# Attention backward for one query row: a broadcast moved into the score bank, the two sums given banks of their own, and the joins of their rows moved one slot later

## The chip, the cores and the metric

The kernel runs on one core of a Trainium2 chip. The metric is device time in microseconds (us), lower is better. Engines: PE (matrix multiply; PEld is its weight load, which overlaps it: in the kernel before 911 us of it beside 1146 us of multiplies, in a span of 1306 us), DVE (vector), ACT (scalar), POOL and SP (here they send the stores and the loads). A "head" is one of the 64 pairs of batch and head; a "slot" is one eighth of a head's work.

## The reference

For each of 64 heads: one query row, 8192 keys and values of length 128, all bf16. Wanted are the forward output and the gradients of q, k and v.

```python
B, H, Sq, Sk, D = 2, 32, 1, 8192, 128

def _fwd_reference(q, k, v):
    scale = q.shape[-1] ** -0.5
    scores = jnp.einsum("bhqd,bhkd->bhqk", q, k) * scale
    p = _softmax(scores, axis=-1)
    return jnp.einsum("bhqk,bhkd->bhqd", p, v)

def reference(q, k, v, grad_out):
    _out, _vjp = jax.vjp(lambda q, k, v: _fwd_reference(q, k, v), q, k, v)   # shortened
    return (_out, *_vjp(grad_out))
```

K and V are read once and their gradients written once: 64 x 2 x 2 MB = 268.5 MB each way. With one query row there is little arithmetic per byte.

## The kernel before

Each slot of head `i` transposes 16 tiles of keys (slots 0 to 3) or values (4 to 7) on PE, copies them out on ACT, and multiplies them with q or the output gradient. Beside it run the previous head's sums (`acc`, PE), the masks that pick the right rows (`pick`, DVE), the join of those rows (`join`, PE, then ACT), and the outer products that make the gradients of k and v (`outer`, DVE), which are then stored. Cuts are marked.

```python
    kvp = ctx.enter_context(tc.tile_pool(name="kv", bufs=6))
    outp = ctx.enter_context(tc.tile_pool(name="outp", bufs=4))
    ps_m = ctx.enter_context(tc.tile_pool(name="ps_m", bufs=2, space=bass.MemoryType.PSUM))
    # ...
    def broadcast(i):                       # q and grad_out of head i on all partitions
        qbp = ps_m.tile([P, 2, D], F32, tag="m", name="qbp")
        pin(nc.tensor.matmul(qbp[:], lhsT=ident_bf[:BH, i : i + 1].to_broadcast([BH, P]),
                             rhs=qd_nat[:], start=True, stop=True))
        h.qb = work.tile([P, 2, D], BF16, tag="qb", name="qb")
        pin(nc.vector.tensor_copy(out=h.qb[:], in_=qbp[:]))
    # ...
    def acc(i, w, c):                       # w=1: values, w=0: keys
        if c == 0:
            h.acc[w] = ps_m.tile([P, QT * D], F32, tag="m", name="acc")
        # ... 4 matmuls of 32 columns x 512
    def pick(i, w): ...                     # DVE: full = acc * diag (0.68 us), sel = reduce(full) (1.04 us)
    def join(i, w): ...                     # PE: acc[:, 0:1] = sel.T @ ones;  ACT: copy to oT / dqT
    # ...
    for g in range(SL * (BH + 2)):          # SL = 8 slots, NCH = 4
        i, s = divmod(g, SL)
        # ... loads
        if live:
            if s == 1: begin_s(i)
            if s == 2: broadcast(i)
            # ...
            ev = transpose_chunk(i, s)
        # ...
        if one: acc(i - 1, 1 if s < NCH else 0, s % NCH)
        if one and s == NCH + 1: join(i - 1, 1)
        if two and s == 1:       join(i - 2, 0)
        # ... scores
        if one and s == NCH: pick(i - 1, 1)
        if two and s == 0:   pick(i - 2, 0)
        # ... outer products: four for each of the two results, then a 2 MB store
```

The broadcast and the two sums share two PSUM banks through one tag. A join stands one slot after its `pick`.

## Time and profile before

| | before |
|---|---|
| time, median of 3 runs | 1306.98 us (1305.65 to 1308.0) |
| PE busy / DVE / ACT | 1146 / 952 / 975 us of a span of 1305.7 |
| bytes moved | 268.5 MB in, 268.5 MB out |
| mean granted PE clock | 0.837 |

From the page of the kernel before: the span in 40 slices (clock in tenths, share of busy DMA engines in tenths, rate), the queues with packets, MB and share of 16 engines, and the chain of work that ended last.

```profile
PEclk9999977788898878778888878689787977886896
DMA  9999999999999999999999999999999999999976
GB/s 375 398 427 428 426 428 427 428 429 425 428 429 427 421 424 424 421 417 422 427 425 422 423 421 406 417 415 427 425 418 425 402 413 411 417 395 423 419 330 266
...
q0 software_dynamic: 18432, 268.44, 49.3%
q1 hardware_dynamic: 19184, 268.51, 48.7%
q8 instruction: 149, 2.44, 0.7%
...
DMA 39%; issue 25%; PE 21%; ACT 10%; DVE 3%; POOL 1%; SPq 0%; POOLq 0%; ACTq 0%
```

The DMA engines are marked busy nearly everywhere; the rate is flat near 428 GB/s at first and ragged later.

Four lines of the list of waits of the kernel before (who waited for whom: total us, times, longest):

```profile
PE acc L337 <- DVE sel L327: 69.5, 109, 4.6
...
PE tp L167 <- DMA kt<-in_k_dram: 39.7, 33, 2.6
...
PE qbp L135 <- ACT dqT L342: 24.0, 62, 0.8
...
PE tp L167 <- DMA vt<-in_v_dram: 9.8, 11, 1.2
```

PE waits 69.5 us for the masks and 24.0 us for the bank in which it puts the broadcast, 93.5 us together, and 49.5 us for loads. The timeline of the kernel before shows both waits of one head (start, duration, instruction, in brackets PE's idle time before it):

```profile
653.22 0.69 DVE L319 TENSOR_TENSOR full<-acc,diag 128x512 f32<-128x512 f32 x1
...
653.95 1.04 DVE L327 TENSOR_REDUCE sel<-full 128x128 f32<-128x512 f32 x1
...
655.04 0.38 PE L337 MATMUL acc<-ones_f,sel 128*128 128x1 f32 x2 [0.59 <-DVE sel L327]
...
655.84 0.28 ACT L342 ACTIVATE dqT<-acc,rls 128x1 bf16<-128x1 f32 x1
...
656.17 0.27 PE L135 MATMUL qbp<-qd_nat,ident_bf 64*128 64x256 bf16 x1 [0.34 <-ACT dqT L342]
```

And longer stretches of it (us, busy time by engine, granted clock, DMA share, GB/s):

```profile
100.00:400.00 300.00, 266.36 (x4526) 212.39 (x4523) 225.32 (x394) 229.99 (x182) 16.52 (x31) 0.86 1.01 428
400.00:700.00 300.00, 270.32 (x4444) 215.01 (x4442) 220.81 (x389) 227.05 (x180) 15.99 (x30) 0.82 1.01 423
700.00:1000.00 300.00, 266.96 (x4422) 212.63 (x4420) 219.07 (x382) 226.73 (x179) 15.46 (x29) 0.84 1.00 419
1000.00:1200.00 200.00, 181.06 (x2918) 143.91 (x2915) 143.00 (x254) 148.05 (x119) 10.67 (x20) 0.80 1.00 411
```

The share stays at 1.0 while the rate sinks from 428 to 411 GB/s.

### The profile page before, as it was taken

To read this page: it belongs to the slowest core of one execution; us is meant where nothing else is said; L and a number is where in the kernel's file an instruction comes from. 1 tells how busy PE (TensorE), PEld (TensorE's weight loads), DVE (VectorE), ACT (ScalarE), POOL (GpSimd) and SP (SyncE) were. 2 spreads that over 40 slices of the span, in tenths; PEclk is the share of its full clock that TensorE was granted. 3 is DMA by queue.
4 is the path that set the end of the run, shared out by engine and by line. 5 is a ranking of instruction groups with operands and counts; after the bars stand their busy time and mean duration, and the time that the engine had idled before them with its cause. 6 is when DMAs were issued, how large, how long until landed. Compare 5 with 4: busy or idle time off the path is not lost.

```text
span 1305.7 us, 41737 instructions
## 1 busy us (share of the span) xinstructions
PE 1146.0 (88%) x19076; PEld 911.5 (70%) x19076; DVE 951.7 (73%) x1680; ACT 974.7 (75%) x769; POOL 69.5 (5%) x136
## 2 busy tenths in 40 slices
PE   7999889999889989999988989988988899999983
PEld 6777777777667777777767767776767677777762
DVE  2888876777777767678777776777676867776776
ACT  7888877787777777768777767778786777876871
POOL 0000000000000000000000000000000000000000
PEclk9999977788898878778888878689787977886896
DMA  9999999999999999999999999999999999999976
GB/s 375 398 427 428 426 428 427 428 429 425 428 429 427 421 424 424 421 417 422 427 425 422 423 421 406 417 415 427 425 418 425 402 413 411 417 395 423 419 330 266
DMA packets 37793, 539.62 MB, mean 413 GB/s; under 512 B 4464, under 2 KB 4464, under 8 KB 4976
## 3 DMA queue, kind: packets, MB, share of 16 engines
q0 software_dynamic: 18432, 268.44, 49.3%
q1 hardware_dynamic: 19184, 268.51, 48.7%
q8 instruction: 149, 2.44, 0.7%
q14 instruction: 28, 0.23, 0.0%
HBM read 268.47 MB, written 268.47 MB: 411 GB/s over the span
## 4 chain that ended last, share of the span: by engine, by line
DMA 39%; issue 25%; PE 21%; ACT 10%; DVE 3%; POOL 1%; SPq 0%; POOLq 0%; ACTq 0%
DMA kt<-in_k_dram 31%; PE tp L167 13%; ACT ev L169 9%; DMA vt<-in_v_dram 8%; PE acc L303 3%; PE sw L179 2%; POOL out_dram L369 1%; PE dpw L179 1%; DVE sel L327 1%; DVE full L319 1%; PE qbp L135 1%; PE acc L337 0%; ACT dqT L342 0%; DVE mp L191 0%; DVE ob L357 0%
## 5 line engine op out<-in xcount | busy, mean ns | idle before, releaser
L169 ACT COPY ev<-tp 128x2048 bf16<-128x2048 bf16 x512 | 939.0, 1871 | 303.9 <-PE tp L167 303.6
L357 DVE TENSOR_TENSOR ob<-qb,pair 128x2048 bf16<-128x2048 bf16 x512 | 611.3, 1216 | 0.0
L167 PE MATMUL tp<-ident_bf,kt 128*128 128x128 bf16 x4096 | 361.6, 259 | 39.7 <-DMA kt<-in_k_dram 39.7
L167 PEld LDWEIGHTS <-kt 128*128 128x128 bf16 x4096 | 311.5, 118 | 80.1 <-DMA kt<-in_k_dram 42.6
L179 PEld LDWEIGHTS <-ev 128*128 128x128 bf16 x8192 | 255.9, 99 | 100.0 <-issue 61.2
L167 PE MATMUL tp<-ident_bf,vt 128*128 128x128 bf16 x4096 | 291.8, 228 | 9.8 <-DMA vt<-in_v_dram 9.8
L167 PEld LDWEIGHTS <-vt 128*128 128x128 bf16 x4096 | 251.0, 103 | 10.8 <-DMA vt<-in_v_dram 10.8
L179 PE MATMUL sw<-qdT,ev 128*128 128x1 bf16 x4096 | 143.5, 165 | 1.0 <-ACT ev L169 1.0
L179 PE MATMUL dpw<-qdT,ev 128*128 128x1 bf16 x4096 | 141.2, 164 | 1.5 <-ACT ev L169 1.5
L191 DVE TENSOR_REDUCE mp<-sw 128x1 f32<-128x64 f32 x64 | 14.4, 225 | 169.9 <-PE sw L179 169.9
L327 DVE TENSOR_REDUCE sel<-full 128x128 f32<-128x512 f32 x128 | 133.1, 1040 | 4.4
L369 POOL DMA_DIRECT2D out_dram<-ob x128 | 68.4, 534 | 1227.8 <-DVE ob L357 637.4
L337 PEld LDWEIGHTS acc<-ones_f,sel 128*128 128x128 f32 x256 | 42.0, 206 | 111.6 <-DVE sel L327 105.5
L337 PE MATMUL acc<-ones_f,sel 128*128 128x1 f32 x256 | 52.8, 276 | 69.9 <-DVE sel L327 69.5
L319 DVE TENSOR_TENSOR full<-acc,diag 128x512 f32<-128x512 f32 x128 | 87.5, 684 | 0.0
L230 DVE CUSTOM_DVE_ANT_0 junk<-E_f,dpw 128x64 bf16<-128x64 f32 x64 | 14.0, 219 | 58.7 <-PE dpw L179 58.7
L303 PE MATMUL acc<-vt,E_pad_110 128*32 128x512 bf16 x336 | 42.7, 499 | 0.0
L303 PE MATMUL acc<-vt,E_pad_109 128*32 128x512 bf16 x352 | 42.3, 473 | 0.0
L135 PE MATMUL qbp<-qd_nat,ident_bf 64*128 64x256 bf16 x64 | 19.6, 307 | 24.0 <-ACT dqT L342 24.0
L303 PE MATMUL acc<-vt,E_pad_111 128*32 128x512 bf16 x336 | 39.7, 463 | 0.0
L303 PE MATMUL acc<-kt,dS_pad_112 128*32 128x512 bf16 x352 | 36.4, 408 | 0.5 <-DVE dS_pad_112 L276 0.5
L303 PE MATMUL acc<-kt,dS_pad_113 128*32 128x512 bf16 x336 | 35.1, 408 | 0.0
(61 smaller groups left out, 458.3 us busy)
## 6 DMA issues: line engine op xcount, KB each, us to landing
out_dram<-ob POOLq DMA_DIRECT2D x128, 2048.0 KB, 28.0
vt<-in_v_dram SPq DMA_DIRECT2D x64, 2048.0 KB, 30.6
kt<-in_k_dram SPq DMA_DIRECT2D x63, 2048.0 KB, 29.2
kt<-in_k_dram SPq DMA_DIRECT2D x4, 512.0 KB, 5.4
qd_nat<-in_q_dram SPq DMA_DIRECT2D x1, 16.0 KB, 1.9
qd_nat<-in_grad_out_dram SPq DMA_DIRECT2D x1, 16.0 KB, 2.0
out_dram<-dqn SPq DMA_DIRECT2D x1, 16.0 KB, 4.9
out_dram<-on SPq DMA_DIRECT2D x1, 16.0 KB, 6.4
```

Of the source, the lines that this page charges most:

```text
L135: nc.tensor.matmul(qbp[:], lhsT=ident_bf[:BH, i : i + 1].to_broadcast([BH, P]), rhs=qd_nat[:], start=True, stop=True,)
L167: pin(nc.tensor.transpose(tp[:, t, :], src[:, n0 + t, :], ident_bf[:]))
L169: pin(nc.scalar.copy(out=ev[:], in_=tp[:]))
L179: nc.tensor.matmul(dst[:, n0 + t : n0 + t + 1], lhsT=ev[:, t, :], rhs=qdT[:, w, i : i + 1], start=True, stop=True,)
L191: pin(nc.vector.reduce_max(out=h.mp[:], in_=h.s, axis=AX.X))
L230: nc.vector.tensor_tensor_reduce(out=junk[:], in0=h.E_f[:], in1=h.dp, scale=1.0, scalar=0.0, op0=ALU.mult, op1=ALU.add, accum_out=h.ld[:, ...
L303: nc.tensor.matmul(h.acc[w][g : g + CW, :], lhsT=wts[:, n0 : n0 + CW], rhs=rows[:, n0 : n0 + QT, :].rearrange("p n d -> p (n d)"), start=( ...
L319: nc.vector.tensor_tensor(out=full[0:NR], in0=h.acc[w][0:NR].rearrange("p (n d) -> p n d", n=QT), in1=diag[0:NR], op=ALU.mult,)
L327: nc.vector.reduce_sum(out=h.sel[0:NR], in_=full[0:NR].rearrange("p n d -> p d n"), axis=AX.X)
L337: nc.tensor.matmul(h.acc[w][:, 0:1], lhsT=h.sel[0:NR], rhs=ones_f[0:NR, 0:1], start=True, stop=True)
L357: nc.vector.tensor_tensor(out=h.ob[:, n0 : n0 + CH, :].rearrange("p n (e t) -> p n e t", t=2), in0=h.qb[:, w, :] .rearrange("p (e t) -> p ...
L369: store_eng.dma_start(out=dst[i], in_=h.ob[:])
```

## The change

Its intent is to take both waits from PE: the broadcast goes into spare columns of the score bank, at slot 0; each sum gets a bank of its own; the joins come two slots after the mask instead of one.

```diff
-    ps_m = ctx.enter_context(tc.tile_pool(name="ps_m", bufs=2, space=bass.MemoryType.PSUM))
+    ps_m = ctx.enter_context(tc.tile_pool(name="ps_m", bufs=1, space=bass.MemoryType.PSUM))
...
-        qbp = ps_m.tile([P, 2, D], F32, tag="m", name="qbp")
         pin(
             nc.tensor.matmul(
-                qbp[:],
+                h.qbp,
...
-        pin(nc.vector.tensor_copy(out=h.qb[:], in_=qbp[:]))
+        pin(nc.vector.tensor_copy(out=h.qb[:], in_=h.qbp))
...
-        sw = ps_sdp.tile([P, NT + P + 1], F32, tag="s", name="sw")
+        sw = ps_sdp.tile([P, NT + P + 1 + 2 * D], F32, tag="s", name="sw")
+        h.qbp = sw[:, NT + P + 1 :].rearrange("p (w d) -> p w d", w=2)
...
-            h.acc[w] = ps_m.tile([P, QT * D], F32, tag="m", name="acc")
+            h.acc[w] = ps_m.tile([P, QT * D], F32, tag=f"acc{w}", name="acc")
...
-            if s == 1:
+            if s == 0:
                 begin_s(i)
-            if s == 2:
                 broadcast(i)
...
-        if one and s == NCH + 1:
+        if one and s == NCH + 2:
             join(i - 1, 1)
-        if two and s == 1:
+        if two and s == 2:
             join(i - 2, 0)
```

(Cut: two helper tiles at the start and the end take the new tags.)

## The prediction

> **What bounds the kernel now.** It moves 268.5 MB in and 268.5 MB out. The page's slices show the DMA engines nine tenths busy or more in 38 of 40; in 50-us windows their share is 0.99 to 1.01 from 50 to 1250 us, at a flat 427 to 428 GB/s from 100 to 400 us. [...] no 50-us window passes 428. So transfers set the pace: at 428 GB/s 537 MB take 1255 us. The rest of the 1306 us is the first 10 us (252 GB/s), a tail of some 48 us after the last head's keys land (stores only, VectorE full, about 20 us of transfer lost), and dips to 406 to 420 GB/s after 500 us (windows 50 to 1250 us average 421: 1.7% of 1200 us, some 20 us).

> PE is second: 88% busy, mean granted clock 0.837, at 0.50 for stretches of some 15 us (205 to 222 us). [...]

> **What the change does.** The list of waits charges PE with 69.5 us for the joins' matmul behind VectorE's "sel" and 24.0 us for the q broadcast behind the ACT copy that frees its bank: 93.5 us, 1.5 us a head. Joining two slots after the mask (a slot is about 2 us at full clock, mask and sum 0.68 + 1.04 us) leaves sel finished when PE arrives; own banks take away the bank wait. No work is added: same matmul (0.27 us) and copy (0.42 us), at slot 0 instead of 2. New dependencies: the broadcast needs the previous head's exponent done (ACT, 0.3 us, ended before that slot in the timeline), and the first score shares its bank with the copy. I expect under 0.3 us a head of new waits.

> **How much is critical.** Little. The chain of waits is 39% DMA, 1.3% sel, 0.7% broadcast. PE's 93 us become mostly longer waits for kt and vt (now 39.7 and 9.8 us): two loads and two stores are already in flight (28 to 32 us to landing). Something returns where loads were issued late: at 1068 us the load queue was nearly empty while PE ran at half clock, and the rate fell to 300 to 360 GB/s in some of the next 15 us. An earlier PE frees buffers sooner: perhaps a quarter to a third of the 20 us of dips, 5 to 7 us. The tail stays.

> **Prediction.** 1301 us, 1287 to 1311 eight times in ten. Faster by over 2% (below 1281 us): 0.05; within 2%: 0.92; slower: 0.03.

> **What would show it right or wrong.**
> - PE's waits on sel and the broadcast's bank: 93.5 us to under 10.
> - PE's waits for kt and vt: 49.5 us to over 100.
> - PE busy nearly unchanged; DMA share 1.0; middle rate 421 to 424 GB/s.
> - Granted clock within 0.04 of 0.837[...].
> - Tail still 45 to 49 us.

> **What would make it wrong.** If the dips come wholly from late loads, the rate rises to 428 and the time falls to about 1285. [...] If the broadcast's copy holds back scores or the maximum, a new wait of 0.5 us a head appears at a head's first scores; DMA would hide most of it.

(Cut from it, where marked, is what no trace or run of this case shows: a ceiling of the transfers, and what lowers the clock. No term of the sum is among them: 1255 us of transfers, the slow start, 20 us in the tail and 20 us of dips make up the 1306 us, and 5 to 7 us of the dips are taken off to give 1301 us.)

## The result, and the profile after

| | before | after |
|---|---|---|
| median (fast runs) | 1306.32 us (4) | 1306.75 us (4) |
| ratio after / before | | 1.0005, 95% interval 0.998 to 1.003 |
| PE busy / span minus PE busy | 1146.0 / 159.7 us | 1144.5 / 159.6 us |
| granted clock | 0.837 | 0.833 |

A ratio is the mean time of one kernel's fast runs over the mean of the other's fast runs of the same rounds, so it is not quite the ratio of the medians. The result is correct, and the time is the same.

The list of waits of the changed kernel, the lines that answer to those of before:

```profile
PE tp L167 <- DMA vt<-in_v_dram: 89.9, 42, 2.7
DVE ob L357 <- DMA out_dram<-ob: 77.4, 80, 1.7
...
PE tp L167 <- DMA kt<-in_k_dram: 41.8, 32, 2.5
...
PE acc L337 <- DVE sel L327: 9.5, 3, 4.8
```

The change did what it was made for: the wait on the mask is 9.5 us (the three that are left are all there is), and the line for the broadcast's bank is gone. PE's waits for loads went from 49.5 to 131.7 us. 84 us left one place and 82 us arrived in another; PE's idle time is the same to a tenth of a microsecond. A new wait shows the same from the other side: DVE now waits 77.4 us for a result buffer whose store has not finished. The timeline of the changed kernel, one join:

```profile
247.46 1.04 DVE L327 TENSOR_REDUCE sel<-full 128x128 f32<-128x512 f32 x1
...
251.88 0.59 PE L337 MATMUL acc<-ones_f,sel 128*128 128x1 f32 x2
...
253.26 0.27 ACT L342 ACTIVATE dqT<-acc,rls 128x1 bf16<-128x1 f32 x1
```

`sel` ends at 248.50 us and the join starts at 251.88 us with no idle time before it. Slices, instruction queue and chain of the changed kernel:

```profile
PEclk9997877787788988877888877877888889787776
DMA  9999999999999999999999999999999999999967
GB/s 374 424 426 427 428 427 427 428 427 429 426 429 427 427 427 419 420 403 424 427 423 424 419 418 416 418 428 422 418 419 407 420 419 417 418 381 425 426 288 298
...
q8 instruction: 149, 2.44, 0.7%
...
DMA 53%; PE 27%; issue 16%; DVE 2%; POOL 1%; ACT 0%; SPq 0%; POOLq 0%; ACTq 0%
```

And its longer stretches:

```profile
100.00:400.00 300.00, 271.03 (x4394) 218.08 (x4392) 220.59 (x386) 226.42 (x177) 15.56 (x30) 0.80 1.01 428
400.00:700.00 300.00, 261.54 (x4431) 209.65 (x4429) 223.11 (x388) 228.54 (x179) 15.94 (x30) 0.85 1.00 422
700.00:1000.00 300.00, 267.63 (x4413) 214.61 (x4411) 220.85 (x385) 226.80 (x178) 15.41 (x29) 0.82 1.01 420
1000.00:1200.00 200.00, 174.74 (x2939) 140.52 (x2939) 147.97 (x256) 151.44 (x119) 10.64 (x20) 0.85 0.99 411
```

The sinking rate is unchanged, stretch by stretch. An earlier PE did not fill the dips. Transfers set the pace of both kernels; but why do they give 1306 us and not the 1255 us that 428 GB/s would?

### The profile page after: what moved, and what is told of

It is laid out like the page before. It is cut to its first block, busy times and chain, and to the rows that moved or that the text cites. A ratio compares the mean times of both kernels' runs of the same rounds, so it can differ in the third digit from the quotient of the medians.

```text
span 1304.1 us, 41737 instructions
## 1 busy us (share of the span) xinstructions
PE 1144.5 (88%) x19076; PEld 918.4 (70%) x19076; DVE 959.9 (74%) x1680; ACT 982.9 (75%) x769; POOL 69.2 (5%) x136
## 3 DMA queue, kind: packets, MB, share of 16 engines
q8 instruction: 149, 2.44, 0.7%
## 4 chain that ended last, share of the span: by engine, by line
DMA 53%; PE 27%; issue 16%; DVE 2%; POOL 1%; ACT 0%; SPq 0%; POOLq 0%; ACTq 0%
DMA vt<-in_v_dram 32%; DMA kt<-in_k_dram 21%; PE tp L167 15%; PE acc L303 5%; PE dpw L179 3%; PE sw L179 2%; PE acc L337 1%; POOL out_dram L369 1%; DVE ob L357 1%; PE sw L201 1%; ACT ev L169 0%; DVE sel L327 0%; PE dpw L244 0%; PE sw L195 0%; DVE full L319 0%
## 5 line engine op out<-in xcount | busy, mean ns | idle before, releaser
L357 DVE TENSOR_TENSOR ob<-qb,pair 128x2048 bf16<-128x2048 bf16 x512 | 610.8, 1216 | 77.4 <-DMA out_dram<-ob 77.4
L167 PE MATMUL tp<-ident_bf,vt 128*128 128x128 bf16 x4096 | 330.9, 246 | 90.1 <-DMA vt<-in_v_dram 89.9
L167 PE MATMUL tp<-ident_bf,kt 128*128 128x128 bf16 x4096 | 324.4, 243 | 41.8 <-DMA kt<-in_k_dram 41.8
L167 PEld LDWEIGHTS <-vt 128*128 128x128 bf16 x4096 | 285.2, 111 | 94.1 <-DMA vt<-in_v_dram 93.5
L179 PEld LDWEIGHTS <-ev 128*128 128x128 bf16 x8192 | 249.9, 99 | 113.3 <-issue 67.4
L167 PEld LDWEIGHTS <-kt 128*128 128x128 bf16 x4096 | 278.7, 110 | 52.5 <-DMA kt<-in_k_dram 48.4
L303 PE MATMUL acc<-kt,dS_pad_112 128*32 128x512 bf16 x352 | 40.2, 452 | 1.3 <-DVE dS_pad_112 L276 1.3
L303 PE MATMUL acc<-vt,E_pad_109 128*32 128x512 bf16 x352 | 38.9, 434 | 0.0
L303 PE MATMUL acc<-vt,E_pad_110 128*32 128x512 bf16 x336 | 38.6, 449 | 0.0
L303 PE MATMUL acc<-vt,E_pad_111 128*32 128x512 bf16 x336 | 38.4, 447 | 0.0
L303 PE MATMUL acc<-kt,dS_pad_113 128*32 128x512 bf16 x336 | 38.0, 443 | 0.0
L303 PE MATMUL acc<-kt,dS_pad_114 128*32 128x512 bf16 x336 | 37.8, 440 | 0.0
```

The lines of the kernel that those rows point to most:

```text
L167: pin(nc.tensor.transpose(tp[:, t, :], src[:, n0 + t, :], ident_bf[:]))
L179: nc.tensor.matmul(dst[:, n0 + t : n0 + t + 1], lhsT=ev[:, t, :], rhs=qdT[:, w, i : i + 1], start=True, stop=True,)
L303: nc.tensor.matmul(h.acc[w][g : g + CW, :], lhsT=wts[:, n0 : n0 + CW], rhs=rows[:, n0 : n0 + QT, :].rearrange("p n d -> p (n d)"), start=( ...
L357: nc.vector.tensor_tensor(out=h.ob[:, n0 : n0 + CH, :].rearrange("p n (e t) -> p n e t", t=2), in0=h.qb[:, w, :] .rearrange("p (e t) -> p ...
```

## The experiments

The theories, with the names that the texts use. **T**: transfers set the pace. **R2**: PE does, and the transfers only look busy. **R3**: waits that the change brings cancel its gain. For the missing 51 us: **R1** and, sharper, **T2**: loads are asked for late, so queues run empty, and the rest is the tail; **R4**: the data traffic of the computing engines slows the transfers; and, formed last, **F**: fetching PE's instructions takes time from one DMA engine. Twelve kernels ran. Each was timed against the kernel before on the same chip, so ratios compare best.

### Is it the transfers? (copy_only)

```diff
-    for g in range(SL * (BH + 2)):
-        # all computation
+    for i in range(BH):
+        store_eng.dma_start(out=dk_v[i], in_=h.kt[:])
+        store_eng.dma_start(out=dv_v[i], in_=h.vt[:])
+        if i + 3 < BH:
+            load_k(i + 3)
+            load_v(i + 3)
```

> All computation removed; the same loads and stores in the same sizes, each store sent from the loaded tile (wrong result on purpose). Theory T (transfers set the pace of both kernels): at 428 GB/s the 537 MB take 1255 us, with the first load's start and the last store's end about 1265 to 1275 us; if the dips to 406 to 420 GB/s after 500 us belong to the transfers themselves, they are here too and the time is 1280 to 1290 us. Rival R1 (loads are issued late because compute frees the buffers late): no dips, a flat 428 GB/s, 1265 us. Rival R2 (PE sets the pace, transfers only look busy): well below 1250 us.

Measured: 1255.64 us, ratio 0.9611 (0.9597 to 0.9626). Longer stretches of copy_only (here there is no ACT column):

```profile
100.00:400.00 300.00, 0.00 (x0) 0.00 (x0) 0.00 (x0) 16.46 (x31) 1.00 1.01 431
400.00:700.00 300.00, 0.00 (x0) 0.00 (x0) 0.00 (x0) 16.47 (x31) 1.00 1.01 431
700.00:1000.00 300.00, 0.00 (x0) 0.00 (x0) 0.00 (x0) 16.47 (x31) 1.00 1.01 431
```

Bare transfers need 1256 us at a flat 431 GB/s, faster than I expected of any theory but R2, and not far enough below 1250 us for that one. So the kernels are 51 us, 4%, above the bare transfers, and the sinking is not in the transfers as such.

### Does the change gain when transfers don't bind? (half_store_before, half_store_after)

Only half of every result is stored, in both kernels, so that the engines set the pace:

```diff
-            store_eng.dma_start(out=dst[i], in_=h.ob[:])
+            store_eng.dma_start(out=dst[i, :, 0 : NT // 2], in_=h.ob[:, 0 : NT // 2])
```

> The kernel before, with only the first half of every result tile stored (403 MB moved in all, 940 us at 428 GB/s; wrong result on purpose). T: with the transfers out of the way the engines set the pace. From the trace a slot at full clock is about 2.0 us, 16.2 us a head, plus 1.46 us of waits on sel and on the bank: about 17.7 us a head, 1100 to 1150 us. R2: stays near 1306 us.

> The changed kernel, same cut of the stores. T: the 93 us of waits that the change removes now count: 1030 to 1080 us, 5 to 8% below half_store_before. Rival R3 (the change brings waits of its own that cancel its gain, whatever the transfers do): equal to half_store_before within 1%.

Measured: 1134.0 us (ratio 0.8666) and 1043.24 us (ratio 0.7986). The change is worth 91 us here, 0.7986 / 0.8666 = 0.92, as T had it. R3 is out: nothing that the change brings cancels it. R2 is out: with PE's work untouched, less to store made the kernel 173 us shorter. Waits of half_store_before:

```profile
PE acc L337 <- DVE sel L327: 83.4, 126, 4.6
...
PE qbp L135 <- ACT dqT L342: 23.3, 62, 0.9
...
PEld L167 <- DMA kt<-in_k_dram: 2.9, 1, 2.9
```

106.7 us of the two waits are in it and almost none for loads. These runs also show what the DMA share is not: a measure of fullness. A stretch of half_store_before, and the line of its page for the loads of v (count, KB each, median us to landing):

```profile
100.00:400.00 300.00, 272.67 (x5255) 218.36 (x5251) 258.77 (x454) 263.94 (x214) 18.61 (x35) 1.00 1.00 372
...
vt<-in_v_dram SPq DMA_DIRECT2D x64, 2048.0 KB, 11.3
```

The share is 1.00 at 372 GB/s, in a kernel that hardly waits for loads. The time from issue to landing tells the two cases apart: 11.3 us here, about 30 us in the two kernels.

### Can a longer PE be paid for from the slack? (after_extra_pe)

```diff
-        for t in range(CH):
+        for t in range(2 * CH if c in (3, 7) else CH):
+            t = t % CH
             pin(nc.tensor.transpose(tp[:, t, :], src[:, n0 + t, :], ident_bf[:]))
```

> The changed kernel with the 16 transposes of two of the eight slots done twice (same result): 32 more transposes a head, 1.05 us for 16 at full clock, so 2.1 us a head, 134 us in all, about what the changed kernel's PE waits for kt and vt (132 us). T: time within 1% of 1306 us, PE's waits for kt and vt down to under 60 us. R2: 60 to 140 us longer. If a PE that idles less keeps a higher clock, the granted clock rises above 0.84 and the added work costs less than that.

Measured: 1313.15 us, ratio 1.005 (1.0023 to 1.0077), correct. Within the 1% of T; R2's 60 us are not there. The clock rose to 0.931, so PE's busy time grew by only 29 us (1173.4 from 1144.5; in the changed kernel 16 transposes took 1.05 us at a granted clock of 1.0 and 1.87 us at 0.50); what raised the clock was not tested apart. The waits for kt and vt fell only to 110 us, not under 60: a miss. A clock 0.1 higher bought nothing either. The 6.5 us (0.5% of 1307) came back as a clue later.

### Which part of the change does the work? (half_store_join_only, half_store_banks_only)

Half the stores again, with one part of the change each:

```diff
 # join_only, from half_store_before
-        if one and s == NCH + 1:      # join(i - 1, 1)
+        if one and s == NCH + 2:
-        if two and s == 1:            # join(i - 2, 0)
+        if two and s == 2:
-            if s == 2:                # broadcast(i)
+            if s == 3:
 # banks_only, from half_store_after
-        if one and s == NCH + 2:      # join(i - 1, 1)
+        if one and s == NCH + 1:
-        if two and s == 2:            # join(i - 2, 0)
+        if two and s == 1:
```

> Half the stores again; of the change only the joins one slot later each; the two shared banks stay (so the broadcast has to go to slot 3, behind the join). In half_store_before PE waited 83 us on sel and 23 us on the bank. Theory T: 70 to 85 us below half_store_before's 1134 us, so 1050 to 1065 us, with the wait on the bank still there or grown. Rival: the banks are what counts, and the joins alone give under 30 us.

> Half the stores; own banks and the broadcast at slot 0, the joins where they were. T: only the 23 us on the bank go: 1105 to 1120 us. Rival: own banks give most of the 91 us.

Measured: 1185.23 us (ratio 0.9068) and 1125.18 us (ratio 0.8603). Against half_store_before's 1134.0 us the banks alone give 9 us; the later joins on top of them give 82 us more (1125.2 to 1043.2); the later joins without them cost 51 us, where I had expected 70 to 85 us of gain. In the timeline of half_store_join_only a part of the reason stands:

```profile
511.98 0.27 ACT L342 ACTIVATE dqT<-acc,rls 128x1 bf16<-128x1 f32 x1
512.30 0.34 PE L135 MATMUL qbp<-qd_nat,ident_bf 64*128 64x256 bf16 x1 [1.13 <-ACT dqT L342]
...
514.55 1.86 ACT L169 COPY ev<-tp 128x2048 bf16<-128x2048 bf16 x1 [2.31 <-PE tp L167]
```

In the shared banks the broadcast must wait for the later join's copy on ACT (70 us in all instead of 23), and then ACT runs dry for 2.31 us. The other part is PE itself: its busy time rose by 76 us (1084.2 from 1008.2) at a granted clock of 0.885 instead of 0.978, and why the clock fell was not tested. So the parts are not additive: the own banks are what makes the later joins possible.

### Are loads and stores asked for too late? (finer_after, finer_before)

Loads and stores of 1 MB, 12 and 8 buffers of half the size; each half is asked for, or sent, as soon as it can be. Core of the edit:

```diff
-    kvp = ctx.enter_context(tc.tile_pool(name="kv", bufs=6))
+    kvp = ctx.enter_context(tc.tile_pool(name="kv", bufs=12))
-    outp = ctx.enter_context(tc.tile_pool(name="outp", bufs=4))
+    outp = ctx.enter_context(tc.tile_pool(name="outp", bufs=8))
...
-        if s == NCH and 1 <= i and i + 2 < BH:
-            load_k(i + 2)
+        if s in (2, 4, 6) and 1 <= i and i + 2 < BH:
+            load_part(i + 2, s // 6, s // 2 % 2 == 0)
...
-        if c == NCH - 1:      # store after four outer products
+        if c % 2:             # store after two
```

> The changed kernel with all stores; loads and stores in halves of 1 MB, twice as many buffers of half the size, so each buffer is asked for and each result sent about two slots (4 us) earlier; same bytes, same result. Theory T2 (the 51 us above the bare transfers' 1256 us are moments when one of the two queues has nothing in it, because buffers come free late, and the tail): 1275 to 1295 us. Rival R4 (compute itself slows the transfers, whatever is queued): only the tail gains, 1299 to 1305 us.

> The kernel before with the same halves. T2: faster than 1306 us too, 1280 to 1300 us; once the queues stay full the change still buys little, so within 1% of finer_after. If PE's 93 us now set the pace, it stays above 1300 us and finer_after is over 1% faster.

Measured: 1320.91 us, ratio 1.0109 (1.0092 to 1.0126), and 1320.14 us, ratio 1.0104 (1.0088 to 1.0119). Both are slower, and T2 failed: loads were now in flight for 36 us on the median (29 to 32 us in the two kernels), so the queues were deeper than before, and the rate still sank, from 424 GB/s (50 to 500 us) to 414 and 410 (1000 to 1200 us). The rate of 50 to 500 us was 424 with transfers of 1 MB in rows of 8 KB, against 426 in the kernel before and 427 in the changed one with 2 MB in rows of 16: lower by 0.5 and 0.7%, where the kernels lost 1.0 and 1.1%; by my estimate from these numbers the rate is about half of the loss. That the two are equal agrees with T.

### A deeper load queue, and a shorter tail (after_seven_in, after_tail)

```diff
 # after_seven_in
-    kvp = ctx.enter_context(tc.tile_pool(name="kv", bufs=6))
+    kvp = ctx.enter_context(tc.tile_pool(name="kv", bufs=7))
-    outp = ctx.enter_context(tc.tile_pool(name="outp", bufs=4))
+    outp = ctx.enter_context(tc.tile_pool(name="outp", bufs=3))
 # after_tail
+        if i == BH - 1:
+            dst = dk_v if w == 0 else dv_v
+            store_eng.dma_start(out=dst[i, :, n0 : n0 + CH], in_=h.ob[:, n0 : n0 + CH])
-        if c == NCH - 1:
+        elif c == NCH - 1:
```

> The changed kernel with seven buffers for loads and three for results instead of six and four (same space, same packets). A load is then asked for about four slots earlier. T2: PE's waits for kt and vt fall from 132 us to under 60, and the time by 5 to 15 us. T (the transfers as such are full): waits move between loads and stores, VectorE waits more for stores than the 77 us of now, and the time stays within 0.5% of 1306 us.

> The changed kernel with the last head's results sent in quarters as they are made. The tail, from the last load's landing to the end, has about 24 us of unused transfer time in the trace; sending the last tile in quarters should give 3 to 5 us: 1301 to 1304 us, the same by the 2% mark but below both kernels.

Measured: 1314.32 us, ratio 1.006 (1.0045 to 1.0075), and 1307.58 us, ratio 1.0003 (0.9988 to 1.0018). The waits moved, as T had it: PE's waits for kt and vt fell from 132 to 3 us, further than T2 had asked, and DVE now waits 209.5 us for stores. So loads were no longer late, and nothing was gained; but the stores had one buffer fewer, so this run alone does not decide against T2. The time grew by a little more than the 0.5% allowed; why is open. Sending the last results sooner gave nothing: the tail was not the loss that I had taken it for.

### Does computation slow the transfers beside it? (copy_and_compute)

The stream of copy_only, and beside it all of the changed kernel's computation on two constant tiles, with no dependence between them (shortened; the result buffers, which are not stored here, go from four to two):

```diff
-        if s == NCH and 1 <= i and i + 2 < BH: load_k(i + 2)
-        if s == 0 and 2 <= i and i + 1 < BH:   load_v(i + 1)
+        if s == 0 and live: move(i)      # store kt, vt; kt, vt = constants; load i + 3
...
-            store_eng.dma_start(out=dst[i], in_=h.ob[:])
```

> The stream of loads and stores of copy_only, and beside it the whole computation of the changed kernel on two constant tiles, with no dependence between the two (wrong result on purpose); about 1040 us of computation beside 1256 us of transfers. Rival R4 (computation slows the transfers that it runs beside): while the engines work, the rate is below 425 GB/s, 1270 to 1285 us. T2 (the dips need transfers that are asked for late): the rate stays at 430 GB/s, 1256 to 1266 us, the latter if the fetching of instructions (2.4 MB in the changed kernel, none in copy_only) costs its share.

Measured: 1307.9 us, ratio 1.001 (0.9994 to 1.0027): the kernels' own time, though no transfer waits for an engine and no engine for a transfer. T2 is finished. R4 had expected 1270 to 1285 us. Stretches of copy_and_compute:

```profile
100.00:400.00 300.00, 296.62 (x5652) 240.47 (x5650) 279.43 (x494) 287.53 (x229) 15.41 (x29) 0.98 1.01 425
400.00:700.00 300.00, 296.09 (x5692) 240.30 (x5689) 281.55 (x499) 289.50 (x230) 15.40 (x29) 0.99 1.00 415
700.00:1000.00 300.00, 295.35 (x5630) 239.38 (x5627) 278.49 (x491) 286.08 (x228) 15.42 (x29) 0.98 1.00 412
```

The rate sinks as in the kernels, and it stays sunk only while the computation lasts (to about 1040 us; in 1100 to 1250 us it was 431 again). But R4 doesn't say why the first 300 us should be spared, when the engines work as hard. A transfer counts as landed when 16 DMA engines have each reported their part, and the trace has those 16 times (4208 reports for 263 transfers in the kernel before). I worked out for every transfer how long the last engine came after the 15th (medians of the transfers that landed in each 100 us):

```
us                      100-200  300-400  500-600  700-800  900-1000
copy_only                   0.3      0.2      0.1      0.3      0.3
copy_and_compute            2.2      6.6     12.1     15.0     15.6
before                      1.2      5.4      9.2     12.8     15.2
after                       1.1      6.1      9.8     13.3     16.5
after_extra_pe              1.2      6.2     10.9     15.8     18.8
half_store_after            0.6      0.4      0.9      0.4      0.8
```

One engine of the 16 falls behind steadily, about 2 us in 100, until it is some 16 us behind. As I read these times, at first the other 15 run ahead into the transfers already asked for, and the total rate stays high. When there are no more transfers to run ahead into, they wait for the one, and the total sinks to its pace. With half the stores it has time to catch up. (In copy_and_compute the median of 500 to 600 us stands between two groups: some 4.5 us, and 19 to 24 us.) What slows one engine? A thing that the kernels have and copy_only lacks is queue q8.

### Is it the fetching of instructions? (copy_and_instructions)

copy_only, and beside it as many PE instructions as the kernels have, on one element each:

```diff
     for i in range(BH):
         h = heads[i]
+        for _ in range(298):
+            pin(nc.tensor.matmul(tiny[:], lhsT=ident_bf[0:1, 0:1], rhs=ident_bf[0:1, 0:1],
+                                 start=True, stop=True))
         store_eng.dma_start(out=dk_v[i], in_=h.kt[:])
```

> The stream of loads and stores of copy_only, and beside it 19072 matmuls of one element by one element on PE, each with its weight load: as many PE instructions as the kernels have (their fetching is the 2.4 MB of the instruction queue), with next to no data read or written by any engine. Theory F (fetching PE's instructions takes time from one of the 16 DMA engines, and every transfer waits for that engine): 1290 to 1310 us, as copy_and_compute; a rate near 427 GB/s at first that falls to 410 to 418 later, and the last of the 16 engines lands further and further behind the 15th, up to 15 to 25 us. Rival R4 (the data that computing engines read and write in the memory slows the transfers): 1256 to 1262 us, a flat 430 GB/s, all engines within 1 us.

Measured: 1307.55 us, ratio 1.0008 (0.9977 to 1.0039). From its page and its stretches:

```profile
q8 instruction: 149, 2.44, 0.7%
```

```profile
100.00:400.00 300.00, 154.88 (x5950) 151.11 (x5950) 0.00 (x0) 15.40 (x29) 1.00 1.01 425
400.00:700.00 300.00, 155.13 (x5960) 151.28 (x5957) 0.00 (x0) 15.40 (x29) 1.00 1.01 417
700.00:1000.00 300.00, 134.34 (x5155) 130.96 (x5154) 0.00 (x0) 15.94 (x30) 1.00 1.01 415
```

One-element matmuls, with DVE and ACT idle, give the whole effect: the time, the sinking, and a last engine that comes 1.5, 6.1, 10.5, 16.5 and 16.5 us after the 15th in the stretches of the table above. R4 is out as the cause: PE's instructions alone are enough. F claims more, that the fetching takes the late engine's time, and the time of the run can't show that. The end of this run shows the straggler by itself; here the 40 slices cover 1200 to 1300 us of copy_and_instructions:

```profile
DMA  9999999999999999999999999999709902980297
GB/s 433 426 419 426 419 433 426 439 433 439 426 413 426 433 426 426 446 433 433 406 433 426 426 387 426 439 403 441 321 33 400 439 26 98 419 347 26 125 420 328
```

Between bursts of the whole group the rate falls to 26 GB/s. One engine's part of 431 GB/s is 431 / 16 = 26.9: one engine is working, and the next store waits for it.

The trace tells more of F. Its DMA packets carry no engine's name, but where one engine works alone, as here, its next packet starts 3 or 4 ns before the recorded end of the one before. So the packets of one engine can often be followed, beginning at the 4-byte packet that reports a landing. From the packet records in the trace file, for 400 to 950 us of copy_and_instructions where no other stretch is named:

- The blocks of q8 do take time from the 16 engines. In the middle of 112 of the 124 blocks between 100 and 900 us, 15 data packets were under way, where 16 is usual. A block took 0.97 us in the mean, a data packet of 16 KB 0.61 us in copy_only.
- They are not the late engine's work. Of its data packets 762 could be followed. If all 85 blocks of that stretch were its own, some 75 would stand among these; none did. Among 3398 packets of the engines that landed 9th to 15th stood 34.
- The late engine's own data packets were longer: 642 ns in the mean, against 611 ns in copy_only. Until PE's last instruction, at 963 us, it moved some 1500 of them (963 us / 642 ns), and 1500 x 31 ns are 47 us: an estimate from these numbers, close to the 52 us lost. From 1000 to 1150 us the mean was 624 ns.

## Why the prediction was right or wrong

The time was right: 1301 predicted, 1306.75 measured, inside 1287 to 1311, and "within 2%" had a chance of 0.92. Point by point:

- **PE's 93.5 us go, to under 10.** Right: 9.5 us are left.
- **They turn into waits for kt and vt, over 100 us.** Right: 131.7 us. This is why so large a saving on PE moved nothing. half_store_after shows that the saving itself is real, 91 us once transfers don't bind.
- **PE busy nearly unchanged, clock within 0.04.** Right: 1144.5 us and 0.833. The traces of both kernels show two levels of the clock, 1.0 and 0.50 (0.50 from 205 to 220 us of the kernel before); what sets the level was not tested.
- **Rate of the middle 421 to 424 GB/s.** Its lower edge: the mean of the 50-us windows from 50 to 1250 us stayed at 421, so nothing was gained.
- **New waits under 0.3 us a head.** Right for the broadcast: its line in the list is 2.0 us in all, of DVE for PE. I did not foresee DVE's 77.4 us for result buffers, which is the same wait for transfers at another place.
- **Tail 45 to 49 us.** Right as a reading: the last head's keys landed at 1257.1 us (issued 1223.85, 33.2 us under way), 47.0 us before the end.
- **"perhaps a quarter to a third of the 20 us of dips, 5 to 7 us", because "loads were issued late".** Wrong, and with it the split of the 1306 us into start, tail and dips. The gain was zero (ratio 1.0005). finer_after, after_seven_in and copy_and_compute each took late loads away in another manner, and none gained. In its place, copy_and_instructions shows a fixed cost: with bare transfers the PE instructions alone add 51.9 us (1307.55 against 1255.64), as much as separates both kernels from the bare transfers.

I expected the tail to hold 20 us of loss of its own. But copy_and_instructions has no computed tail, and its time is the same. Its end is ragged as well, for the slow engine has its backlog to finish. after_tail's zero agrees.

The number of instructions fits: the kernels have 19076 matmuls and as many weight loads, and their q8 has 149 packets of 16 KB (2.44 MB): 38152 / 149 = 256 PE instructions for each. 51.9 us over 149 blocks are 0.35 us of delay for each 256 instructions. after_extra_pe has 165 packets, so 16 x 0.35 = 5.6 us more are to be expected, an estimate from these two numbers, and it lost 6.5 us (3 to 10 us by its interval). This cannot tell the fetching from anything else that grows with the number of PE instructions.

What stays open: I have shown that one engine lags and that PE instructions cause it, but not how. The packets speak against the blocks: the late engine carries none that could be found, and 149 blocks of 0.97 us on one engine would be 145 us, nearly three times the loss. A rival that no run here tests is the recording of the instructions. Every timed run lists a granted clock, so each was recorded as it ran: copy_only with 585 instructions, copy_and_instructions with 38729, the kernels with 41737. If the recording is what slows that engine, the 52 us belong to it and not to the kernel; timing copy_only and copy_and_instructions without it would tell. No version beat both kernels. The one lever left, fewer PE instructions for the same transposes and scores, was not tried.

## What to carry to other kernels

Before spending work on an engine's waits, measure the floor with a copy of the kernel that only loads and stores, and a second that cuts the stores in half: the first tells how much there is to gain (51 us here), the second whether your saving is real (91 us here). A DMA share of 1.0 proved nothing by itself (it was 1.00 at 372 GB/s in half_store_before); times to landing did better (11.3 us there, about 30 us in the two kernels), and the uneven landing of the 16 engines, the last up to 18.8 us behind the 15th, showed a bottleneck that the share hid. Beside transfers near their limit, the PE instructions cost 51.9 us of transfer time in copy_and_instructions, though PE was busy for only 497 of its 1305 us. These runs were all recorded; that it is so without the recording is not shown.
